# Stores of one weight's sums moved to SyncE's queue, and ScalarE taking over copies and scalings at the end of the plain tile

## The chip, the cores and the metric

The kernel runs on one core of one Trainium2 chip. A core has TensorE (PE, matmuls), VectorE (DVE), ScalarE (ACT), GpSimd (POOL) and SyncE (SP), each with an instruction stream of its own that is worked through in order. In this kernel SP and ACT issue the DMA transfers. The metric is the device time of one execution in microseconds (us), as the median of several runs.

## What is computed

Retention attention without softmax, and then a SwiGLU feed-forward block:

```python
q, k, v: (8, 8, 576, 64)          # batch, heads, tokens, head size
scores = scale * q @ k^T
ret = scores * gamma[h] ** (i - j)   for j <= i, else 0
attn = ret @ v
x = attn, heads beside each other:   (4608, 512)
g = x @ w_gate;  val = x @ w_val     # 512 x 1536 each
out = (silu(g) * val) @ w_out        # 1536 x 512
```

Everything is float32.

## The kernel before

**Attention.** Heads are worked on in pairs, 4 pairs (HP) to a batch entry, 32 pairs in all. `tick(t)` advances three pairs at once: it loads nothing itself, but transposes pair t (`transposes`), makes scores, states and masks of pair t - 1 (`scores`, `new_states`, `masked`), and values of pair t - 2 (`own_values`, `earlier_values`), which `to_x` writes into x, transposed. The parts on VectorE and ScalarE are put on the list `pieces` and taken off by `go_on(n)` between other work, so their place in the order of VectorE and ScalarE is set by hand. For a pair i,

- `light(i)` says that q is scaled ahead (by ScalarE, `scale_q`, L480), so that `to_x` only has to copy (ScalarE, L595 and L617); otherwise `to_x` multiplies by a table (VectorE, L597 and L611);
- `vector(i)` says that the keys are scaled by VectorE (L498) and that `even`, a copy of the states' first half out of PSUM, is made by VectorE (L571) for the pair before; otherwise ScalarE does both (L500, L571).

`needed(1)` is 14 and `needed(2)` is 22, so `light` holds for pairs 12 to 19, and `vector` for pairs 0, 10, 11 and 12.

**The plain tile.** The first 512 tokens go through the feed-forward block with plain matmuls: `up0` (12 blocks of 128 columns of w_gate and w_val, silu on ScalarE, product on VectorE) and `down0` (12 steps m, four matmuls each on the four PSUM banks A, B, C, E; L707). At m = 1, 3, 6 and 8 of `down0` the ticks 10 to 13 stand. They finish pairs 8 to 11. At the end `out0` copies the four banks (L712; A and B by ScalarE, C and E by VectorE) and stores them.

**The other four tiles.** Each has 1024 tokens and is multiplied by a fast scheme with 26 products (tables UP and DOWN) in place of 32 block products. Its operands are sums and differences of blocks of x, of the weights and of the hidden layer. One product is a *step*. `up_step(n, qd, i)` is step i of tile n with quarter qd of the hidden columns (NQ = 3). In tile 1 ("busy") the sums of the weights are made in passing (`w_sums`, GpSimd and ScalarE) and stored in DRAM by ScalarE's queue (L942), for the later tiles to fetch. The results of a step are read out of the bank by `reads`: a copy by ScalarE (L875), or a sum by VectorE (L878), and then silu (L954) and product (L957, L960, L961). A bank must have been read before the step that uses it next; the banks rotate by `rested`.

**Sums of x** (`x_sums`, L729 by way of `add`). Table UP has 21 of them. For tile 1 VectorE makes 14 ahead of step 0 (X_FIRST_OF_ALL: six at m = 9 and 10 of `down0`, the rest behind `out0`), and one more at each step from step 0. For the later tiles it is 8 ahead (X_FIRST). They are written to `xsum`, buffers that lie where earlier work had its own.

**Sums of w_out** (`out_sums(qd)`, L722 to L729). The 26 combinations of w_out's blocks (OUT_SUMS), 128 x 256 for each qd, are made and stored in DRAM tensors dn0 to dn25. GpSimd makes qd 0 and 1, and its stores are issued by SP. VectorE makes qd 2, and the first 18 of its stores are issued by ScalarE's queue (L790). Of its last eight, two that need no buffer follow there (L811), and six are issued by SP after the loop (`late_stores`, L792). Each qd is cut into nine groups of three stores. GpSimd's first 12 groups stand between the `up0` blocks. From m = 0 of `down0`, each m issues one group of GpSimd's (qd 1, groups 4 to 9) and then one of VectorE's (groups 1 to 9). A sum takes the first free buffer of its list; a buffer goes back to the end of the list when its sum is stored or no longer used, and whoever takes it again waits until the store has landed. VectorE's list (`vector_places`) has 22 buffers, of which the first eight (x0) are never given back.

A store waits on its queue until its sum is there, and every later instruction of that queue waits behind it.

Of the kernel before, what the change touches and what calls it, by code (L numbers as in the profile page):

```python
# [154 lines left out]
def kernel(  # L155
# [32 lines left out]
    nc = tc.nc  # L188
# [13 lines left out]
    TB = TW // 4  # L202
    NF = DF // P
    NQ = NF // 4
# [52 lines left out]
    def needed(n):  # L257

        last = (min(starts[n] + TW, NT) - 1) // S
        return last * HP + HP - 1 + 3  # L260
# [186 lines left out]

    def light(i):

        return needed(1) - 2 <= i < needed(2) - 2  # L450

    def vector(i):

        return i == 0 or 10 <= i <= needed(1) - 2

    def transposes(i):
        p = i % HP
        qk, kn, vt = loaded.pop(i)
        qT = early[i] if i < HP else qp.tile([P, S], F32, tag="qT", name="qT")
        st[i] = dict(qT=qT, kn=kn, v=vt)  # L460
        pieces = []

        copy = nc.scalar.copy if i else nc.vector.tensor_copy
        if i < HP:

            for n, (t, src, bank) in enumerate(((kT, kn, bankB), (qT, qk, bankA)) if i else ((qT, qk, bankA), (kT, kn, bankB))):
                for c in range(NFULL):
                    nc.tensor.transpose(bank[:, ts(c, P)], src[:, ts(c, P)], ident)
                for hl in range(2):
                    nc.tensor.matmul(bankC[half[hl], ts(n, L)], src[half[hl], CW : CW + D], ident[half[hl], half[hl]],  # L470
                                     start=True, stop=True, skip_group_check=True)
                copy(t[:, 0:CW], bank)
                copy(t[:, CW:S], bankC[:, ts(n, L)])
        else:
            if light(i):
                def scale_q():

                    src = qk[:, 0].rearrange("p (j r) d -> p r j d", r=2)
                    for r in range(2):
                        nc.scalar.activation(out=src[:, r], in_=src[:, r], func=AF.Copy, scale=piece[:, 2 * p + r : 2 * p + r + 1])  # L480
                pieces.append(scale_q)
            for n, t in enumerate((qT, kT)):
                pieces.append(lambda n=n, t=t: nc.vector.transpose(out=t, in_=qk[:, n].rearrange("p j d -> p (j d)")))

        every = slice(0, P)

        def keys():
            blocks = kn.rearrange("p (g d) -> p g d", d=D)
            if i < HP:
                parts = [(0, every, blocks[:, 0 : NC - 1 : 2]), (1, every, blocks[:, 1:NC:2]), (1, half[1], blocks[half[1], NC - 1])]  # L490
            elif whole(i):
                parts = [(0, every, blocks[:, 0:NFULL]), (1, every, blocks[:, NFULL:NC])]
            else:
                parts = [(hl, every, blocks[:, hl : 2 * NFULL : 2]) for hl in range(2)]
            for hl, rows, at in parts:
                scale = key[rows, 2 * p + hl : 2 * p + hl + 1]
                if vector(i) or 1 < i < HP:
                    (nc.vector if vector(i) else nc.gpsimd).tensor_scalar(out=at, in0=at, scalar1=scale, scalar2=None, op0=ALU.mult)  # L498
                else:
                    nc.scalar.activation(out=at, in_=at, func=AF.Copy, scale=scale)  # L500

        if light(i):
            return [lambda: (keys(), pieces[0]())] + pieces[1:]
        if vector(i) and i:
            return [lambda: None] + pieces + [keys]
        return [keys] + pieces

    straight, exchanged = [(slice(0, P), slice(0, P))], [(half[0], half[1]), (half[1], half[0])]
# [127 lines left out]
    pieces = []  # L636

    def tick(t, lo=HP, hi=NP, spread=False, then=None):
        go_on(len(pieces))
        if hi == HP:  # L640

            if lo <= t - 1 < hi:
                scores(t - 1, True)
                new_states(t - 1)
                for f in masked(t - 1):
                    f()
            if t + 1 == HP:
                split(0)
                rounding(0)
            if lo <= t - 2 < hi:  # L650
                own_values(t - 2)
            for f in transposes(t) if lo <= t < hi else ():
                f()
            if t + 1 == HP:
                rounding(1)
            if lo <= t - 2 < hi:
                earlier_values(t - 2)
                to_x(t - 2)[0]()
            return
        if lo <= t - 2 < hi:  # L660
            own_values(t - 2)
        if lo <= t - 1 < hi:
            new_states(t - 1)
        if lo <= t - 2 < hi:
            earlier_values(t - 2)
        if lo <= t - 1 < hi:
            scores(t - 1, t - 2 < lo)
        if lo <= t - 1 < hi and whole(t - 2) and not whole(t - 1):
            decay(slice(0, H), slice(0, H), half[1])
        copies, *masks = masked(t - 1) if lo <= t - 1 < hi else (lambda: None,)  # L670
        keys, *new = transposes(t) if lo <= t < hi else (lambda: None,)
        outputs = to_x(t - 2)[0] if lo <= t - 2 < hi else lambda: None
        if t - 2 >= 0 and light(t - 2):
            pieces.append(lambda: (copies(), keys(), outputs()))
        else:
            pieces.extend([lambda: (copies(), keys()), outputs])
        pieces.extend(masks)
        pieces.extend(new)
        if then:
            pieces.append(then)  # L680
        if not spread:
            go_on(len(pieces))
# [26 lines left out]

    def out0():  # L710
        for i, (bank, o) in enumerate(zip(banks, (hid0[f] for f in (0, 1, 4, 5)), strict=True)):
            (nc.vector.tensor_copy if i > 1 else nc.scalar.copy)(out=o, in_=bank)  # L712
            nc.sync.dma_start(out=out[i * P : (i + 1) * P, :], in_=o)


# [16 lines left out]
    dn_ops = [dr.tile([P, 768], F32, name=f"dn{i}") for i in range(N)]  # L732
# [16 lines left out]
    def out_sums(qd):  # L749
# [6 lines left out]
            if not any(p is q for q in x0_places):  # L756
                sum_places.append(p)

        eng, queue, sum_places = ((nc.vector, nc.scalar, vector_places) if qd + 1 == NQ else (nc.gpsimd, nc.sync, pool_places))

        def view(s):
            return w_dn[:, qd, s // 2, s % 2] if s < 8 else place[s]
# [21 lines left out]
        def do(k):  # L784
            e = events[k]
            if e[0] is None:
                _, slot, i = e
                to, what = dn_ops[i][:, qd * TB : (qd + 1) * TB], view(slot)
                if stored[k] < on_time:
                    queue.dma_start(out=to, in_=what)  # L790
                elif slot > 7:
                    late_stores.append(lambda: nc.sync.dma_start(out=to, in_=what))  # L792
            else:
                new = sum_places.pop(0)
                add(eng, e[1], view, new)
                if e[0] in place:
                    free(place[e[0]])
                place[e[0]] = new
            release(k)
# [3 lines left out]
        for g in range(0, N, 3):  # L803
            lo, hi = ends[g - 1] + 1 if g else 0, ends[min(g + 2, N - 1)] + 1

            def group(lo=lo, hi=hi):
                for k in range(lo, hi):
                    do(k)
                    if stored[k] + 1 == on_time and events[k][0] is None:
                        for _, slot, i in [e for e in events[k + 1 :] if e[0] is None and e[1] < 8]:  # L810
                            queue.dma_start(out=dn_ops[i][:, qd * TB : (qd + 1) * TB], in_=view(slot))  # L811

            r.append(group)
        return r
# [74 lines left out]

    x_ops = [op for line in up for op in line[3]]  # L890
    X_FIRST = 8
    X_FIRST_OF_ALL = 14

    def x_sums(n, lo, hi, vector):
        for op in x_ops[lo:hi]:
            add(nc.vector if vector or op[0] == "nad" else nc.gpsimd, op, x_view(n))
# [25 lines left out]
    def up_step(n, qd, i):  # L922
        label, opens, xslot, _, wslot, _, ops = up[i]
        busy = n == 1
        if qd == 0:
            first = X_FIRST_OF_ALL if busy else X_FIRST
            x_sums(n, first + i, first + i + 1, busy)
        if busy:
            if i > 1:
                w_sums(qd, i)  # L930
# [125 lines left out]
    for m, f in enumerate(down_order):  # L1056
        down0(f)
        go_on(6)
        if m in tick_at:
            tick(tick_at[m], HP, FIRST, tick_at[m] + 1 < needed(1))  # L1060
            go_on(1)
        if m == 5:
            first_sums(0, 0, 1)
        if m == 8:
            first_sums(0, 1, 4)
        if 8 < m < 11:
            x_sums(1, 3 * (m - 9), 3 * (m - 8), True)
        if groups:
            groups.pop(0)[1]()
        if last_groups:  # L1070
            last_groups.pop(0)()
    for store in late_stores:
        store()
    out0()
    x_sums(1, 6, X_FIRST_OF_ALL, True)
    done = FIRST

    def spread_tick(t):
# [56 lines left out]
```

## Time and profile before

| | us |
|---|---|
| median of 3 runs | 1063.14 (1060.99 to 1063.37) |
| the profiled execution | 1060.99 |
| its span, first to last instruction | 1059.3 |

The page's second part cuts the span into 40 slices of 26.5 us and gives each engine's busy tenths:

```profile
PE   6999999999999999999999999999999999999998
PEld 5554555788788888888888888888888888888887
DVE  5568789786878667454467787426375554244644
ACT  4456401232533211231322112232220022222110
POOL 2002358565455107622224038412250383122505
```

The plain tile's `down0` lies at 128 to 181 us (slices 5 and 6, counted from 0), and step 0 of tile 1 starts at 180.3 us. A row of the timeline gives the start, the length, the engine, the source line and the operation of one instruction or of several alike ("x3") and, in brackets, how long the engine had been idle and what ended it; "SPq" and "ACTq" are DMA issues of those queues. Line numbers are those of the kernel before.

### The profile page before, as it was taken

Reading aid. Unit: us, or ns where it says so; the run is one execution under the profiler, and the core shown is the slowest. Engines: PE = TensorE matmul, PEld = TensorE weight load, DVE = VectorE, ACT = ScalarE, POOL = GpSimd, SP = SyncE. Lnnn points to the kernel's source line nnn. Section 1 sums busy time; section 2 is a strip of 40 time slices with the busy share of each in tenths; the row PEclk is TensorE's granted clock in tenths of the full one; section 3 lists DMA queues with packets and bytes.
Section 4 is the critical chain, followed back from the end, with each engine's and each line's share of the span. In section 5 each row is a group of like instructions: output and inputs, shape, how many; then the busy total and the mean of one; then the engine's idle time right before and its main releaser. Section 6 shows DMA issues by size and latency. Waiting matters only on the chain.

```text
span 1059.3 us, 21436 instructions
## 1 busy us (share of the span) xinstructions
PE 1037.8 (98%) x8448; PEld 849.5 (80%) x8448; DVE 660.9 (62%) x1094; ACT 273.4 (26%) x579; POOL 390.9 (37%) x338
## 2 busy tenths in 40 slices
PE   6999999999999999999999999999999999999998
PEld 5554555788788888888888888888888888888887
DVE  5568789786878667454467787426375554244644
ACT  4456401232533211231322112232220022222110
POOL 2002358565455107622224038412250383122505
PEclk9999999999999999999999999999999999999999
DMA  9998786676768869765666777544554555555553
GB/s 263 248 258 239 191 247 216 185 199 187 196 175 215 265 166 257 199 149 175 190 183 172 212 197 212 152 147 141 153 179 150 154 187 151 151 155 160 181 159 99
DMA packets 305083, 199.09 MB, mean 188 GB/s; under 512 B 219992, under 2 KB 248664, under 8 KB 304984
## 3 DMA queue, kind: packets, MB, share of 16 engines
q1 hardware_dynamic: 270968, 159.02, 54.7%
q10 hardware_dynamic: 34016, 38.71, 10.9%
q8 instruction: 67, 1.10, 0.4%
q14 instruction: 32, 0.26, 0.1%
HBM read 157.56 MB, written 40.11 MB: 187 GB/s over the span
## 4 chain that ended last, share of the span: by engine, by line
PE 73%; DVE 5%; issue 1%; POOL 1%; DMA 1%; ACT 0%; SPq 0%; DVEq 0%; ACTq 0%; POOLq 0%
PE bankC L938 12%; PE bankE L938 11%; PE bankB L938 11%; PE bankA L938 11%; PE bankA L978 6%; PE bankE L978 6%; PE bankB L978 6%; PE bankC L978 6%; DVE rest L878 2%; PE outer L546 1%; PE outer L521 1%; PE inner L560 1%; PE inner L531 1%; DVE arena L960 1%; DVE arena L957 1%
## 5 line engine op out<-in xcount | busy, mean ns | idle before, releaser
L878 POOL TENSOR_TENSOR rest<-rest 128x512 f32<-128x512 f32 x56 | 79.2, 1419 | 297.7 <-DVE rest L878 279.2
L954 ACT ACTIVATE io<-rest 128x256 f32<-128x256 f32 x180 | 75.0, 416 | 343.7 <-DVE rest L878 292.1
L938 PE MATMUL bankA<-rest,arena 128*128 128x256 f32 x544 | 129.0, 380 | 1.0 <-DVE rest L878 1.0
L938 PE MATMUL bankC<-rest,arena 128*128 128x256 f32 x544 | 129.2, 380 | 0.5 <-DVE rest L878 0.5
L938 PE MATMUL bankB<-rest,arena 128*128 128x256 f32 x512 | 121.5, 380 | 2.0 <-POOL arena L907 1.6
L729 POOL TENSOR_TENSOR arena<-arena 128x512 f32<-128x512 f32 (+1 forms) x72 | 113.8, 1593 | 24.4 <-DMA up<-arena 11.5
L938 PE MATMUL bankE<-rest,arena 128*128 128x256 f32 x512 | 121.4, 380 | 0.6 <-DVE rest L878 0.6
L938 PEld LDWEIGHTS bankA<-rest,arena 128*128 128x128 f32 x544 | 102.9, 190 | 16.5 <-issue 1.4
L938 PEld LDWEIGHTS bankC<-rest,arena 128*128 128x128 f32 x544 | 102.8, 190 | 15.5 <-issue 1.2
L961 POOL TENSOR_TENSOR arena<-rest,io 128x256 f32<-128x256 f32 x72 | 51.8, 726 | 167.5 <-ACT io L954 167.5
L938 PEld LDWEIGHTS bankB<-rest,arena 128*128 128x128 f32 x512 | 96.9, 190 | 16.3 <-POOL arena L907 2.4
L938 PEld LDWEIGHTS bankE<-rest,arena 128*128 128x128 f32 x512 | 96.9, 190 | 14.6 <-DVE rest L878 1.0
L729 POOL TENSOR_TENSOR rest<-rest 128x256 f32<-128x256 f32 (+1 forms) x66 | 67.6, 1044 | 105.6 <-DVE rest L417 62.8
L878 DVE TENSOR_TENSOR rest<-bankC,rest 128x512 f32<-128x512 f32 x72 | 48.8, 686 | 67.4 <-PE bankC L938 47.2
L878 DVE TENSOR_TENSOR rest<-bankB,rest 128x512 f32<-128x512 f32 x72 | 48.9, 687 | 64.9 <-PE bankB L938 46.9
L878 DVE TENSOR_TENSOR rest<-bankE,rest 128x512 f32<-128x512 f32 x72 | 48.8, 686 | 64.4 <-PE bankE L938 46.3
L878 DVE TENSOR_TENSOR rest<-bankA,rest 128x512 f32<-128x512 f32 x72 | 48.8, 685 | 63.5 <-PE bankA L938 45.9
L957 DVE SCALAR_TENSOR_TENSOR arena<-rest,io 128x256 f32<-128x256 f32 x84 | 56.1, 673 | 11.7 <-ACT io L954 11.2
L978 PE MATMUL bankA<-arena 128*128 128x256 f32 x252 | 58.0, 380 | 1.4 <-DVE arena L729 1.4
L978 PE MATMUL bankB<-arena 128*128 128x256 f32 x252 | 58.3, 381 | 0.0
L978 PE MATMUL bankC<-arena 128*128 128x256 f32 x252 | 58.1, 380 | 0.0
L978 PE MATMUL bankE<-arena 128*128 128x256 f32 x252 | 57.9, 379 | 0.0
(184 smaller groups left out, 1626.6 us busy)
## 6 DMA issues: line engine op xcount, KB each, us to landing
arena<-up SPq DMA_DIRECT2D x234, 256.0 KB
arena<-dn SPq DMA_DIRECT2D x104, 384.0 KB
up<-arena ACTq DMA_DIRECT2D x78, 256.0 KB
out_dram<-rest SPq DMA_DIRECT2D x32, 256.0 KB
qk<-in_q_dram SPq DMA_DIRECT2D x108, 72.0 KB
qk<-in_k_dram SPq DMA_DIRECT2D x108, 72.0 KB
dn<-rest SPq DMA_DIRECT2D x58, 128.0 KB
rest<-in_moe_w_out_dram ACTq DMA_DIRECT2D x6, 1024.0 KB
```

What stands on the lines that cost most here:

```text
L521: m = nc.tensor.matmul(xo[half[hl ^ r * exchange(i)], c, r], s["v"][rows, at], ret[rows, r if whole(i) else hl, c], start=(c == 0), stop=( ...
L531: nc.tensor.matmul(z[half[hl], r, c], s["kn"][chunk(i, hl, 2 * c + r, i < HP)], s["v"][rows, at], start=True, stop=True, skip_group_check= ...
L546: nc.tensor.matmul(xr[half[hl]] if c + 1 == NC else xo[half[hl ^ c % 2 * exchange(i)], c // 2, c % 2], state[half[hl], c, :], s["qT"][half ...
L560: nc.tensor.matmul(sc[chunk(i, hl, 2 * c + r)[0], r if whole(i) else hl, c], kT[half[hl], at], qT[half[hl], at], start=True, stop=True, sk ...
L729: eng.tensor_tensor(out=dst, in0=srcs[0], in1=srcs[1], op=ALU.add if op[0] == "add" else ALU.subtract)
L878: eng.tensor_tensor(out=at(op[1]), in0=at(op[2]), in1=at(op[3]), op=ALU.add if op[0] == "add" else ALU.subtract)
L938: m = nc.tensor.matmul(b[:, gv * TB : (gv + 1) * TB], w[:, gv, ts(c, P)], rhs[:, c, :], start=(opens and gv == 0 and c == 0), stop=(c == 1 ...
L954: nc.scalar.activation(out=s, in_=src[:, 0:TB], func=AF.Silu, scale=-1.0 if negative else 1.0)
L957: return lambda: nc.vector.scalar_tensor_tensor(out=dst, in0=src[:, TB : 2 * TB], scalar=-1.0, in1=s, op0=ALU.mult, op1=ALU.mult)
L960: return lambda: nc.vector.tensor_tensor(out=dst, in0=src[:, TB : 2 * TB], in1=s, op=ALU.mult)
L961: nc.gpsimd.tensor_tensor(out=dst, in0=src[:, TB : 2 * TB], in1=s, op=ALU.mult)
L978: nc.tensor.matmul(b[:, m * TB : (m + 1) * TB], lhs[:, qd, ts(m, P)], w[:, qd], start=(opens and qd == 0 and m == 0), stop=(qd == NQ - 1), ...
```

## The change

- `light` holds from pair 8 in place of 12: q of pairs 8 to 11 is scaled by ScalarE, and their x is copied by ScalarE.
- `vector` holds for pair 0 alone: keys of pairs 10 to 12 are scaled by ScalarE, and `even` is copied by ScalarE in ticks 10 to 12.
- In ticks 10 and 11 (`late`) the order of the pieces is: the copy of `even` with the outputs, the masks, then keys and the scaling of q, then the transposes.
- `out0` copies all four banks by ScalarE.
- All stores of w_out's sums, VectorE's too, are issued by SP.
- For tile 1, 8 sums of x stand ahead of step 0 (at m = 9, 10 and 11) in place of 14; step i makes the (9 + i)th.

```diff
     def light(i):
-        return needed(1) - 2 <= i < needed(2) - 2
+        return needed(1) - 6 <= i < needed(2) - 2

     def vector(i):
-        return i == 0 or 10 <= i <= needed(1) - 2
+        return i == 0
...
         if light(i):
             return [lambda: (keys(), pieces[0]())] + pieces[1:]
-        if vector(i) and i:
-            return [lambda: None] + pieces + [keys]
         return [keys] + pieces
...
         outputs = to_x(t - 2)[0] if lo <= t - 2 < hi else lambda: None
-        if t - 2 >= 0 and light(t - 2):
+        late = needed(1) - 4 <= t < needed(1) - 2
+        if late:
+            pieces.append(lambda: (copies(), outputs()))
+        elif light(t - 2):
             pieces.append(lambda: (copies(), keys(), outputs()))
         else:
             pieces.extend([lambda: (copies(), keys()), outputs])
         pieces.extend(masks)
+        if late:
+            pieces.append(keys)
         pieces.extend(new)
...
         for i, (bank, o) in enumerate(zip(banks, (hid0[f] for f in (0, 1, 4, 5)), strict=True)):
-            (nc.vector.tensor_copy if i > 1 else nc.scalar.copy)(out=o, in_=bank)
+            nc.scalar.copy(out=o, in_=bank)
             nc.sync.dma_start(out=out[i * P : (i + 1) * P, :], in_=o)
...
-        eng, queue, sum_places = ((nc.vector, nc.scalar, vector_places) if qd + 1 == NQ else (nc.gpsimd, nc.sync, pool_places))
+        eng, sum_places = (nc.vector, vector_places) if qd + 1 == NQ else (nc.gpsimd, pool_places)
...
                 if stored[k] < on_time:
-                    queue.dma_start(out=to, in_=what)
+                    nc.sync.dma_start(out=to, in_=what)
...
                         for _, slot, i in [e for e in events[k + 1 :] if e[0] is None and e[1] < 8]:
-                            queue.dma_start(out=dn_ops[i][:, qd * TB : (qd + 1) * TB], in_=view(slot))
+                            nc.sync.dma_start(out=dn_ops[i][:, qd * TB : (qd + 1) * TB], in_=view(slot))
...
     X_FIRST = 8
-    X_FIRST_OF_ALL = 14
...
         if qd == 0:
-            first = X_FIRST_OF_ALL if busy else X_FIRST
-            x_sums(n, first + i, first + i + 1, busy)
+            x_sums(n, X_FIRST + i, X_FIRST + i + 1, busy)
...
-        if 8 < m < 11:
-            x_sums(1, 3 * (m - 9), 3 * (m - 8), True)
+        if m > 8:
+            x_sums(1, 3 * (m - 9), min(3 * (m - 8), X_FIRST), True)
...
     for store in late_stores:
         store()
     out0()
-    x_sums(1, 6, X_FIRST_OF_ALL, True)
     done = FIRST
```

## The prediction

> **What bounds the kernel now.** I read the shares of the page first, then the busy time by stretch, then the timeline around the end of the plain tile, then the waits.
>
> ```profile
> PE 1037.8 (98%) x8448; PEld 849.5 (80%) x8448; DVE 660.9 (62%) x1094; ACT 273.4 (26%) x579; POOL 390.9 (37%) x338
> ```
>
> TensorE is the bound: 21.5 us of the span are idle, and the change leaves TensorE's instructions as they are. What the change can win is idle time of PE, what it can lose is new idle time. The stretches around it (us busy for PE, PEld, DVE, ACT, POOL, then granted clock):
>
> ```profile
> 125.00:150.00 25.00, 25.00 (x448) 14.99 (x447) 19.62 (x47) 1.23 (x3) 10.41 (x13) 1.00 0.83 201
> 150.00:175.00 25.00, 24.91 (x252) 13.01 (x251) 22.43 (x49) 1.26 (x2) 23.18 (x30) 1.00 0.60 201
> 175.00:200.00 25.00, 23.14 (x92) 17.04 (x91) 24.74 (x29) 7.18 (x14) 12.88 (x9) 1.00 0.61 201
> ```
>
> PE is full until 175, and from 150 to 200 VectorE is full as well, while ScalarE is nearly empty. So the plain tile's end is PE's, the start of step one is VectorE's. The timeline shows the second:
>
> ```profile
> 180.32 1.89 PE L938 MATMUL bankA<-rest,arena 128*128 128x256 f32 x8
> ...
> 192.00 0.68 DVE L878 TENSOR_TENSOR rest<-bankA,rest 128x512 f32<-128x512 f32 x1
> ...
> 195.83 1.99 PE L938 MATMUL bankB<-rest,arena 128*128 128x256 f32 x8 [1.04 <-POOL arena L907]
> ...
> 198.40 1.99 PE L938 MATMUL bankE<-rest,arena 128*128 128x256 f32 x8 [0.57 <-DVE rest L878]
> ```
>
> Steps follow each other at 1.73 us (180.32, 182.05, 183.78 in the rows between). Step 4's bank A is complete at 187.23 + 1.89 = 189.1, but DVE reads it at 192.00, 2.9 us late, since sums of x and two bank copies stand ahead of it. Step 9 should start at 180.32 + 9 x 1.73 = 195.9 and starts at 198.40: 2.5 us are lost. That is the prize.
>
> The stores of w_out's sums now go out on two queues:
>
> ```profile
> 135.35 23.80 ACTq L790 DMA_DIRECT2D dn<-rest  x15
> ...
> 161.10 3.98 ACTq L790 DMA_DIRECT2D dn<-rest  x3
> 165.33 0.84 ACTq L811 DMA_DIRECT2D dn<-rest  x2
> ```
> ```profile
> 165.33 11.95 SPq L790 DMA_DIRECT2D dn<-rest  x15
> ```
> ```profile
> SPq L790 <- POOL rest L729: 14.1, 21, 1.9
> ```
>
> The ACT queue's 20 are VectorE's quarter (qd 2), issued as each sum is ready. SP's are GpSimd's, and SP sits waiting for GpSimd's sums, in order: 21 waits, 14.1 us. The 15 from 165.33 are GpSimd's 12th to 26th of qd 1 (dn11 first).
>
> **The change, part by part.**
>
> *ScalarE for VectorE.* DVE sheds the outputs of four ticks (the L597 and L611 rows from 164.52 to 165.45, 0.93 us each: 3.7), three copies of `even` (0.42: 1.2), the key scalings of pairs 10 and 11 (1.28 + 1.16) and of pair 12 (1.2), and two bank copies (0.68 each: 1.4), some 10 us. ACT takes them: per pair 0.35 (even), about 0.9 (x), 0.96 (keys), 0.95 (q scaled, L480), and 0.58 a bank, some 12.5 us in a stretch where it is busy 1.2 us of 25. Cost: nothing, hidden by that idle time. PE doesn't gain before 175 either, since it is full there. One thing slips: the first store of step one's weights (178.87, behind the copy of bank B) now stands behind the copy of bank E, which PE ends at 180.5: 1.7 us late. GpSimd's sum at 183.52 waits for it and is due at step 6 (190.7), so 5.9 us of cover take it in; without cover it costs 1.7.
>
> *Fewer sums of x ahead.* Six sums (0.69 us alone, 1.39 beside a busy GpSimd) leave the place before step 4's reading sum; with the bank copies that is 6 x 0.69 + 1.4 = 5.5 us against 2.9 us of lateness, so the 2.5 us can be won. They come back at steps 4 to 12: DVE then has 8 reading sums and 9 sums of x (17 x 0.69) and 5 products (0.42), 13.8 us, in 9 x 1.73 = 15.6 us. It fits if GpSimd doesn't stretch it; rows of 1.47 and 1.75 us in that stretch say that some are. Gain 0 to 2.5; I take 2.0.
>
> *All stores by SP.* This is where I expect the loss. In program order each m of the down loop issues one group of GpSimd's sums (qd 1, groups 4 to 9) and then one of VectorE's (groups 1 to 6), so on SP's queue VectorE's first group (dn14, dn2, dn9), ready at 135 to 139, now stands behind GpSimd's dn11, which is issued at 165.33. Why it matters: `vector_places` has 22 buffers. Counted through OUT_SUMS, VectorE's 23rd sum takes the first one freed, the one that held dn6 (third group), and must wait until dn6's store has landed; the 24th waits for dn3's. Now dn6 leaves on ACT at 146.57, and the 23rd sum runs unhindered at 163.76, the last of this row; behind it on DVE stand the masks and states of pair 11, which PE needs for the last tick:
>
> ```profile
> 161.37 3.23 DVE L729 TENSOR_TENSOR rest<-rest 128x256 f32<-128x256 f32 x4
> ...
> 165.45 0.68 DVE L567 TENSOR_TENSOR ret<-inner,near 128x512 f32<-128x512 f32 x1
> ...
> 167.94 0.69 PE L521 MATMUL outer<-ret,v 64*64 64x64 f32 x32
> ...
> 168.89 1.10 PE L546 MATMUL outer<-qT,state 64*64 64x64 f32 x32
> ```
>
> After: dn6 is the 14th store behind dn11 on SP (3 + 3 GpSimd + 3 + 3 GpSimd + dn1, dn6). Pace of a queue with nothing to wait for: 0.84/2 = 0.42 us (L811) to 3.19/6 = 0.53 (L792). 14 x 0.48 = 6.7: issued at 172.0; GpSimd's dn8, two ahead, is ready at about 170.8 (the second sum of the row at 169.39), so it asks for no more. Landing: a store issued at 150.09 let GpSimd go on at 153.1, 3.0 us (up to 4.65 for the larger store of 178.87 to 183.52). So the 23rd sum starts at 175.0 in place of 163.76. From there to PE's L546 it took 168.89 - 163.76 = 5.1 us, of which 0.9 were outputs that ACT now makes: 4.2. PE's L546 starts at 179.2, 10.3 us later; the two steps of down0 ahead of it end at 167.2 and nothing else can run on PE meanwhile. [...] Stall: 9.3, bounds 5 (0.42 a store, 2 us to land, GpSimd 2 us early) and 15 (0.75 a store, as the slowest of the L792 ones, and 4.65). Against a gain: below 0 only if the store isn't waited for.
>
> *Clock.* A pause of PE has a tail in this trace:
>
> ```profile
> 24.08 0.33 PE L470 MATMUL bankC<-ident,rest 64*64 64x64 f32 x4 [2.49 <-ACT kT L473]
> ```
> ```profile
> 25.00:30.00 5.00, 5.00 (x23) 2.30 (x20) 3.01 (x8) 3.16 (x6) 0.00 (x0) 0.66 0.89 302
> ```
>
> After 2.49 us of idle PE ran at 0.66 of its clock for 5 us: 0.34 x 5 = 1.7 us of work lost. I add 1.7 once (0 to 2.5). [...]
>
> **Sum**, from the profiled execution's 1060.99 us (span 1059.3 and 1.7 around it): + 9.3 (stall) + 1.7 (clock) - 2.0 (steps 7 to 9) = + 9.0, so 1070.0. The median of the runs shown is 2.15 above that execution: 1072; I say 1071, the pace of the stores being more likely nearer to 0.42.
>
> **Rivals.**
> 1. *The store is not in the way* (faster): dn6 lands before DVE comes to its 23rd sum. Price: - 2.5 and up to 1.1 more from the pauses at 218.47 and 222.72 (0.60 and 0.53 idle): about 1060. It decides if GpSimd has dn8 ready by about 160, ten us sooner than its row says. For it: GpSimd stood still for 14.1 us until 143.2, waiting for a store that was behind loads on SP. Against: those loads are still there, and from 143 it works without a break. Chance 0.08.
> 2. *Half of it* (within 0.3%, 1060.0 to 1066.3, about what a measurement can tell from no change): GpSimd is 3 us earlier, landing takes 2 us, the stall is 5, no clock is lost, 2.5 to 3.5 come back: 1065. Chance 0.13.
> 3. *Worse*: with 35 stores in a row the DMA is the bound, 0.75 a store: 14 x 0.75 + 4.65 puts the 23rd sum at 180.5, the stall at 15: 1078. For it: the last two of the six L792 stores took 0.56 and 0.75. Against: 0.60 to 0.61 DMA share in these stretches. Chance 0.14.
>
> **How the numbers follow.** My forecast, a stall of 6 to 12 us, has 0.65. With rival 3, slower by over 0.3% has 0.79; same 0.13; faster 0.08. The range 1064.5 to 1077 leaves out rival 1, a part of 2 and the end of 3.
>
> **What would show it.** Right: DVE's row of w_out sums has an idle time of some 10 us ended by the DMA of dn<-rest, L567's mask after it at about 176, PE idle for 8 us or more ahead of the last tick's matmuls (the `state` ones), a clock under 1.00 in the stretch behind it, and step 9 at 9 x 1.73 us behind step 0. No store of dn stands on ACT's queue. Wrong: the last tick's PE work at 168 to 170 as now; then the mapping of buffer to store is my error. If step 9 still comes late, the sums of x moved back are what VectorE can't fit.

## The result, and the profile after

The changed kernel takes 1068.27 us (median of 4 runs, 1066.08 to 1069.96) against 1062.84 for the kernel before beside it (4 runs, 1060.99 to 1063.37). The ratio is 1.0053, 95% interval 1.0029 to 1.0077: slower by 5.4 us, where 1071.0 was forecast. A second comparison of the same two kernels, made with the experiments, gave 1.0053 again (1.0035 to 1.0072). The profiled execution is the one of 1066.08 us, span 1064.4, 5.1 us over that of the profile before.

The page's shares:

```profile
PE 1039.6 (98%) x8448; PEld 851.7 (80%) x8448; DVE 650.6 (61%) x1063; ACT 284.4 (27%) x610; POOL 389.3 (37%) x338
```

VectorE has 31 instructions fewer, ScalarE 31 more: the takeover is there. TensorE does the same 8448 matmuls in 1.8 us more busy time, so part of the loss isn't idle time. The stretches (us busy for PE, PEld, DVE, ACT, POOL, then granted clock, DMA share, GB/s):

```profile
150.00:175.00 25.00, 19.68 (x232) 11.01 (x232) 11.30 (x22) 1.04 (x4) 20.45 (x27) 0.92 0.60 199
175.00:200.00 25.00, 25.00 (x94) 16.81 (x91) 13.30 (x18) 8.78 (x18) 6.58 (x6) 0.94 0.55 194
200.00:225.00 25.00, 24.44 (x113) 20.83 (x112) 23.77 (x30) 6.29 (x13) 20.50 (x14) 1.00 0.75 198
```

From 150 to 175 PE is idle for 5.3 us where it was full, VectorE has fallen from 22.4 busy to 11.3, and the clock is 0.92 and then 0.94. VectorE does less here, and still PE waits for it. The timeline says why:

```profile
154.78 22.95 SPq L793 DMA_DIRECT2D dn<-rest  x39
165.54 1.02 PE L710 MATMUL bankE<-rest,arena 128*128 128x512 f32 x2
170.53 0.42 DVE L732 TENSOR_TENSOR rest<-rest 128x256 f32<-128x256 f32 x1 [12.90 <-DMA dn<-rest]
170.88 0.68 DVE L565 TENSOR_TENSOR ret<-inner,near 128x512 f32<-128x512 f32 x1
171.75 1.14 PE L519 MATMUL outer<-ret,v 64*64 64x64 f32 x32 [5.18 <-DVE ret_last L573]
173.49 1.98 PE L544 MATMUL outer<-qT,state 64*64 64x64 f32 x32
175.40 2.07 PE L710 MATMUL bankA<-rest,arena 128*128 128x512 f32 x2
187.11 1.89 PE L939 MATMUL bankA<-rest,arena 128*128 128x256 f32 x8
196.01 0.69 DVE L881 TENSOR_TENSOR rest<-bankA,rest 128x512 f32<-128x512 f32 x1 [10.27 <-PE bankA L939]
```

SP issues 39 stores of dn from 154.78 to 177.7. The single sum at 170.53 is VectorE's 23rd: it has waited for 12.90 us, for a dn store to land. Behind it stand the masks (L565) and `ret_last`, and PE, out of work since 166.6, waits for them for 5.18 us. After the pause matmuls run slower: L544 takes 1.98 us where it took 1.10, two of L710 take 2.07 where they take 1.02 at 165.54. The granted clock is 0.50 from 173.4 to 177.4, 0.84 in the 2 us behind that and 1.00 from 179.4.

With the matmuls of the two traces laid side by side, the 5.1 us are made up so:

| where | us |
|---|---|
| start-up, before 31 us | - 1.45 |
| from there to L544, 168.89 before and 173.49 now: the pause | + 6.05 |
| L544 to step 0 (180.32 and 187.11): the clock | + 2.2 |
| step 0 to step 9 (18.08 us before, 15.54 now): VectorE's and GpSimd's lateness is gone | - 2.54 |
| later pauses of PE, 0.56 and 1.51 us ahead of steps 13 and 22, less those of before (the rest of the 5.1) | + 0.85 |

The start-up is the same code, and in the second profile of this kernel it is only 0.42 us earlier, so the first row is a matter of the execution.

### The profile page after: what moved, and what is told of

It is laid out like the page before. It is cut to its first block, busy times and chain, and to the rows that moved or that the text cites. A ratio compares the mean times of both kernels' runs of the same rounds, so it can differ in the third digit from the quotient of the medians.

```text
span 1064.4 us, 21448 instructions
## 1 busy us (share of the span) xinstructions
PE 1039.6 (98%) x8448; PEld 851.7 (80%) x8448; DVE 650.6 (61%) x1063; ACT 284.4 (27%) x610; POOL 389.3 (37%) x338
## 4 chain that ended last, share of the span: by engine, by line
PE 84%; DVE 5%; POOL 3%; issue 3%; DMA 2%; SPq 1%; ACT 1%; ACTq 0%; DVEq 0%; POOLq 0%
PE bankC L939 11%; PE bankE L939 11%; PE bankA L939 11%; PE bankB L939 11%; PE bankA L979 6%; PE bankB L979 6%; PE bankC L979 6%; PE bankE L979 6%; PE bankA L698 2%; PE bankC L698 2%; PE outer L544 2%; PE bankB L698 2%; PE bankE L698 2%; PE outer L519 2%; DVE rest L881 2%
```

## The experiments

All times are medians beside runs of the kernel before on the same chip, which took 1061.23, 1062.2 and 1062.41 us in the three sets; ratios are to those.

**1. VectorE's stores back on ScalarE's queue, all else as changed.**

```diff
-        eng, sum_places = (nc.vector, vector_places) if qd + 1 == NQ else (nc.gpsimd, pool_places)
+        eng, queue, sum_places = (nc.vector, nc.scalar, vector_places) if qd + 1 == NQ else (nc.gpsimd, nc.sync, pool_places)
...
-                    nc.sync.dma_start(out=to, in_=what)
+                    queue.dma_start(out=to, in_=what)
```

> The changed kernel with VectorE's stores of w_out's sums back on ScalarE's queue. Theory (the 23rd sum waits for dn6's store behind GpSimd's stores on SyncE, PE's last tick stalls, the clock falls): no idle of PE ahead of the last tick, clock 1.00 at 150 to 200, time 1059 to 1061.5, below the kernel before. Rival A (the spread sums of x or ScalarE's new work cost the time): 1066 to 1069 as the changed kernel. Rival B (crowded DMA on SyncE's queue, whatever the buffer): as the theory, 1059 to 1061.5.

Measured: 1067.43 us, ratio 1.0058 (1.0042 to 1.0075). That is the time of the changed kernel, and what rival A had said (1066 to 1069); my theory and rival B, which had 1059 to 1061.5, missed. The wait for dn6 is gone, and another has come, by way of ScalarE's new work. From the timeline:

```profile
163.41 2.25 ACTq L793 DMA_DIRECT2D dn<-rest  x3
166.33 0.81 ACTq L814 DMA_DIRECT2D dn<-rest  x2
167.24 0.37 ACT L569 COPY even<-inner 128x256 f32<-128x256 f32 x1 [5.87 <-DMA dn<-rest]
167.64 0.69 DVE L565 TENSOR_TENSOR ret<-inner,near 128x512 f32<-128x512 f32 x1 [4.46 <-ACT even L569]
172.09 1.97 PE L544 MATMUL outer<-qT,state 64*64 64x64 f32 x32 [2.39 <-DVE state L580]
```

ScalarE's copy of `even`, the work that it has taken over, stands in ScalarE's order behind five stores, and those wait in that same order. VectorE had ended its sums at 163.2, 4.46 us ahead of the mask at 167.64, so the last of these stores no longer waited for a sum; what the profile names as the end of ScalarE's idle time is the landing of a store. VectorE's masks wait for the copy, PE for the masks (1.27 us at L519) and the state. What was to be a control of one part joined two parts of the change that don't go together; run 5 takes that apart.

**2. All stores by SP alone, on the kernel before.**

```diff
-        eng, queue, sum_places = ((nc.vector, nc.scalar, vector_places) if qd + 1 == NQ else (nc.gpsimd, nc.sync, pool_places))
+        eng, queue, sum_places = ((nc.vector, nc.sync, vector_places) if qd + 1 == NQ else (nc.gpsimd, nc.sync, pool_places))
```

> The kernel before with VectorE's stores on SyncE's queue and nothing else. Theory: the stall appears, 5 to 8 us idle of PE at the last tick, 2 us of clock, nothing won back: 1068 to 1072. Rival A: as the kernel before, within 1.5 us of it. Rival B: as the theory.

Measured: 1069.87 us, ratio 1.0082 (1.0065 to 1.0099). The timeline, and then the clock of the two stretches:

```profile
174.82 0.44 DVE L729 TENSOR_TENSOR rest<-rest 128x256 f32<-128x256 f32 x1 [10.70 <-DMA dn<-rest]
176.97 1.13 PE L521 MATMUL outer<-ret,v 64*64 64x64 f32 x32 [8.61 <-DVE ret_last L575]
```
```profile
150.00:175.00 25.00, 18.36 (x172) 9.05 (x171) 12.78 (x27) 0.00 (x0) 22.73 (x29) 0.94 0.54 180
175.00:200.00 25.00, 22.89 (x130) 15.25 (x131) 19.84 (x37) 4.98 (x9) 5.89 (x4) 0.85 0.62 213
```

The one line of the queue makes the same wait, with a longer pause of PE, 8.61 us in the profiled execution (1073.34 us, the longest of the six), and costs 8.6 us in the median. Nothing comes back: step 9 is at 209.51, 17.68 us behind step 0 (191.83).

**3. Another buffer for the 23rd sum.** A buffer that is overwritten by a later sum is taken again first. The 23rd sum then takes the one of dn5, whose late store has not read it yet, so in this run a third of dn5 holds another sum; the work is the same.

```diff
                 if e[0] in place:
-                    free(place[e[0]])
+                    if qd + 1 == NQ and not any(place[e[0]] is q for q in x0_places):
+                        sum_places.insert(0, place[e[0]])
+                    else:
+                        free(place[e[0]])
```

> The changed kernel, all stores on SyncE, but the one freed buffer that is never stored is taken again first, so that the 23rd sum finds a fresh buffer and only the 24th (behind the masks) waits for dn6. Theory: the stall is gone although the queue is as crowded: 1059 to 1062. Rival A: 1066 to 1069. Rival B: 1066 to 1069, since the stores are as late as before.

Measured: 1060.27 us, ratio 0.9993 (0.9981 to 1.0006). No pause of PE at the last tick, clock 0.999, step 0 at 178.72:

```profile
166.34 0.69 PE L519 MATMUL outer<-ret,v 64*64 64x64 f32 x32
167.29 1.10 PE L544 MATMUL outer<-qT,state 64*64 64x64 f32 x32
```

All stores still stand on SP's queue, so it isn't their number that costs.

**4. The spread of the sums of x alone, on the kernel before.**

```diff
-            first = X_FIRST_OF_ALL if busy else X_FIRST
-            x_sums(n, first + i, first + i + 1, busy)
+            x_sums(n, X_FIRST + i, X_FIRST + i + 1, busy)
```

(and, as in the change, nothing behind `out0` and two more at m = 11)

> The kernel before with 8 sums of x ahead of step one in place of 14 and nothing else. Theory: step 9 no longer late by 2.5 us but VectorE fuller at steps 4 to 12: between -2.5 and +1 us against before, 1060.5 to 1064. Rival A: slower by 3 us or more.

Measured: 1060.7 us, ratio 0.9999 (0.9987 to 1.0012): no change that could be told. VectorE reads step 4's bank 3.5 us sooner than before (188.48), and step 9 comes on time, at 195.13, 15.5 behind step 0. About half of what that earns goes again at steps 13, 18 and 22; step 22 starts 41.07 us behind step 0, against 42.40 in the kernel before (PE's idle times in the timeline):

```profile
202.83 1.97 PE L936 MATMUL bankE<-rest,arena 128*128 128x256 f32 x8 [0.56 <-DVE rest L878]
212.19 1.99 PE L936 MATMUL bankA<-x_odd,arena 128*128 128x256 f32 x8 [0.49 <-POOL arena L906]
220.66 1.97 PE L936 MATMUL bankC<-rest,arena 128*128 128x256 f32 x8 [1.27 <-DVE rest L878]
```

**5. ScalarE's takeover alone, on the kernel before** (the changes of `light`, `vector`, the ticks and `out0`; stores and sums of x as before).

```diff
-        return needed(1) - 2 <= i < needed(2) - 2
+        return needed(1) - 6 <= i < needed(2) - 2
...
-        return i == 0 or 10 <= i <= needed(1) - 2
+        return i == 0
```

> The kernel before with only ScalarE's part: ticks 8 to 11 light (q scaled by ScalarE in front of its product, keys by GpSimd, the two copies to x by ScalarE) and all four evictions of the early output by ScalarE; VectorE's tile's stores stay on ScalarE's queue and 14 sums of x stay ahead. My theory: the added work of ScalarE stands in its order behind stores that wait for VectorE's sums and for a place in the DMA queue, so ScalarE's copy (L569 or near it) in the last tick waits as in e1, PE pauses 3 to 6 us at about 165 to 172, and the time is 1064 to 1069 us. Rival, the takeover is free as I had forecast, and e1's loss comes from the spread of x's sums: 1059 to 1062 us, no pause of PE over 1.5 us between 150 and 175.

Measured: 1064.67 us, ratio 1.0021 (1.0007 to 1.0034): my theory, at its lower end. (The keys, which the expectation gives to GpSimd, are scaled by ScalarE, L500. What it calls a wait for a place in the DMA queue is seen as this: VectorE had ended its sums at 163.0, stores were still issued at 165.22 and 166.35, and the profile names the landing of a dn store as the end of ScalarE's 6.11 us.) The timeline shows the same row as in run 1:

```profile
166.35 0.83 ACTq L814 DMA_DIRECT2D dn<-rest  x2
167.28 0.37 ACT L569 COPY even<-inner 128x256 f32<-128x256 f32 x1 [6.11 <-DMA dn<-rest]
168.63 0.69 PE L519 MATMUL outer<-ret,v 64*64 64x64 f32 x32 [1.66 <-DVE ret_last L573]
172.08 1.97 PE L544 MATMUL outer<-qT,state 64*64 64x64 f32 x32 [2.34 <-DVE state L580]
```

PE idles 1.66 + 2.34 = 4.0 us. Steps 0 to 9 then follow without lateness (185.88 to 201.41, 15.53 us) although 14 sums of x stand ahead.

**6. The changed kernel with the 10th sum's buffer taken again first.** That value is never stored, so nobody waits for it; the 23rd sum gets the last unused buffer, the 24th the one of dn6.

```diff
+                kept.append(what)
...
                 if e[0] in place:
-                    free(place[e[0]])
+                    old = place[e[0]]
+                    if qd + 1 == NQ and not any(old is q for q in x0_places + kept):
+                        sum_places.insert(0, old)
+                    else:
+                        free(old)
```

> The changed kernel; VectorE's sums of the last quarter take again first the buffer whose value was never stored (that of the 10th sum). The 23rd sum then takes the last unused buffer and waits for nothing; the 24th, one group later, takes the one of dn6. My theory: what is behind the 24th sum is only sums of x for step one onwards, which have slack, so it costs at most 1 us: 1059.5 to 1062.5 us, PE without a pause over 1 us before its state product L544. Rival, the wait only moves: the 24th sum holds the sums of x until about 171 and step 0 to 4 come late: 1063 to 1066 us.

Measured: 1060.9 us, ratio 0.9984 (0.997 to 0.9997). The timeline:

```profile
155.10 24.89 SPq L794 DMA_DIRECT2D dn<-rest  x42
162.68 0.69 DVE L565 TENSOR_TENSOR ret<-inner,near 128x512 f32<-128x512 f32 x1 [2.13 <-ACT even L569]
169.15 0.69 PE L519 MATMUL outer<-ret,v 64*64 64x64 f32 x32
170.09 1.10 PE L544 MATMUL outer<-qT,state 64*64 64x64 f32 x32
173.20 0.90 DVE L732 TENSOR_TENSOR rest<-rest 128x256 f32<-128x256 f32 x1 [7.17 <-DMA dn<-rest]
```

The store is as late as before and VectorE still waits for it, 7.17 us. But the waiting sum now stands behind the masks, PE goes through the tick without a pause, and L544 keeps its 1.10 us. A wait of the same kind costs some 7 us in one place of VectorE's order and nothing in the next.

**7. Run 2 with the buffers of run 6**: the kernel before, all stores by SP, no takeover.

> The kernel before with the last quarter's stores on SP's queue, as in e2, and the same order of buffers as in e6. My theory: on SP's queue the stores harm by the one buffer that VectorE waits for, and by nothing else: 1060 to 1064 us, where e2 took 1069.9. Rival, a crowded queue of SP as such (loads and stores behind the stores come late): 1066 to 1070 us.

Measured: 1063.6 us, ratio 1.0006 (0.9992 to 1.002), where run 2 had 1.0082. The timeline:

```profile
171.06 1.15 PE L546 MATMUL outer<-qT,state 64*64 64x64 f32 x32 [0.48 <-DVE state L582]
172.68 1.09 DVE L729 TENSOR_TENSOR rest<-rest 128x256 f32<-128x256 f32 x1 [1.68 <-DMA dn<-rest]
```

On SP's queue the stores harm by that wait and by nothing that can be measured; the interval leaves room for 2 us.

**8. Run 6 with 14 sums of x ahead, as before.**

```diff
+    X_FIRST_OF_ALL = 14
...
-            x_sums(n, X_FIRST + i, X_FIRST + i + 1, busy)
+            first = X_FIRST_OF_ALL if busy else X_FIRST
+            x_sums(n, first + i, first + i + 1, busy)
```

> e6 with 14 sums of x ahead of step one, as in the kernel before, in place of 8 and one a step. In e3 VectorE idled for 5.3 us just before it read step 4's bank, and was then late at some steps from 9 on (pauses of PE of 0.7 to 1.5 us). If those 6 sums fill that idle time, the gain of spreading them isn't needed and the pauses at steps 12 to 22 fall away: 1057.5 to 1060.5 us. Rival: the sums wait for x's loads or for buffers, hold VectorE's read of step 4, and cost what they save: 1060.5 to 1063.5 us.

Measured: 1060.08 us, ratio 0.9977 (0.9964 to 0.999). It is faster than both kernels, by 0.23% than before and by some 0.75% than the changed one. The two stretches that the prediction read show where the room is: VectorE, busy 22.43 and 24.74 us of 25 in the kernel before, now has 17.99 and 22.77.

```profile
150.00:175.00 25.00, 24.91 (x251) 12.90 (x250) 17.99 (x27) 3.31 (x11) 23.27 (x29) 1.00 0.63 207
175.00:200.00 25.00, 24.51 (x101) 18.69 (x100) 22.77 (x29) 8.56 (x16) 11.37 (x9) 1.00 0.77 247
```

Against run 6 it is 0.8 us, within the intervals: whether 8 or 14 stand ahead can't be told apart.

**9. One store moved.** In the changed kernel, dn6's store of VectorE's quarter alone goes back to ScalarE's queue.

```diff
-                    nc.sync.dma_start(out=to, in_=what)
+                    (nc.scalar if qd + 1 == NQ and i == 6 else nc.sync).dma_start(out=to, in_=what)
```

> The changed kernel; of VectorE's 20 stores that moved, dn6's alone goes back to ScalarE's queue, and no buffer is given in another order. My theory, that the loss is the wait of the 23rd sum for this one store: 1060 to 1063 us, as e6, and no pause of PE over 1 us ahead of L544. Rival, that other stores behind GpSimd's on SP's queue cost something too, or that ScalarE is held up by this one store: 1064 to 1068 us.

Measured: 1061.31 us, ratio 0.9991 (0.9977 to 1.0006), beside 1.0053 for the changed kernel in the same set. One DMA issue of 0.36 us, in another queue, takes some 6.6 us off. The rows of that store and of the next sum that waits:

```profile
144.61 0.36 ACTq L793 DMA_DIRECT2D dn<-rest  x1
174.25 0.83 DVE L732 TENSOR_TENSOR rest<-rest 128x256 f32<-128x256 f32 x1 [8.71 <-DMA dn<-rest]
```

dn6 leaves at 144.61 instead of 168.37. The 24th sum waits for dn3's store, 8.71 us, and that costs nothing, as in run 6.

**10. The changed kernel with 14 sums of x ahead** (the edit of run 8), and **11. the changed kernel again**.

> The changed kernel with 14 sums of x ahead of step one, so without its third part. If the spread is worth nothing with the pause in place, as e4 showed without it: the same as the run of the changed kernel beside it, within 1 us (1067 to 1069). If the spread costs time where steps come late, as the difference of e1 (ratio 1.0058) to e5 (1.0021) would have it: 2 to 3 us faster than the changed kernel (1064.5 to 1066.5). If it earns the 2.0 us of my forecast: 2 us slower (1070).

> The changed kernel once more, for a comparison on the same chip with the two runs beside it: 1066 to 1069.5 us, ratio 1.004 to 1.007. A wait of VectorE of 10 to 14 us for a dn store ahead of its last tick's masks, and PE idle for 4 to 7 us at L519.

Measured: 1067.08 us, ratio 1.0047 (1.0029 to 1.0065), and 1068.04 us, 1.0053 (1.0035 to 1.0072): the spread is worth nothing that could be told beside the pause either. From the timeline of run 10, and then of run 11:

```profile
172.88 0.42 DVE L732 TENSOR_TENSOR rest<-rest 128x256 f32<-128x256 f32 x1 [12.95 <-DMA dn<-rest]
174.10 1.13 PE L519 MATMUL outer<-ret,v 64*64 64x64 f32 x32 [5.24 <-DVE ret_last L573]
```
```profile
171.54 0.49 DVE L732 TENSOR_TENSOR rest<-rest 128x256 f32<-128x256 f32 x1 [12.72 <-DMA dn<-rest]
172.81 1.13 PE L519 MATMUL outer<-ret,v 64*64 64x64 f32 x32 [5.22 <-DVE ret_last L573]
```

Three profiles, three times the same pause of 5.2 us. The gap between run 1 and run 5 (1.0058 and 1.0021), which differ by the spread alone, is thereby not explained by it. They were measured in different sets, their profiled executions hardly differ (1065.27 and 1064.99 us, PE's two pauses 3.66 and 4.0 us together), and it stays open.

## Why the prediction came out as it did

**The stall: right in place and cause.** The 23rd sum waits for dn6's store, the 14th behind dn11 on SP, and the last tick's masks stand behind it. Runs 2, 6, 7 and 9 show it from four sides: the queue alone makes the stall, another buffer takes it away with the queue left as it is, with or without the takeover, and so does the one store. That the DMA is not the bound (rival 3) is shown by run 3 and run 6, where a row of stores as long (42 in the line of run 6) costs nothing (ratios 0.9993 and 0.9984). Rival 1 fell with the wait of 12.90 us. Rival 2 had a landing of 2 us and GpSimd 3 us sooner, near to what came (2.16 us, and dn11 out 4.1 us sooner, 1.45 of it start-up), but no loss of clock and 2.5 to 3.5 us won back; the 2.2 of the clock and the 1.7 won back are what sets the result apart from it. Its stall of 5 us is a wrong sum: its own terms give 165.33 - 3 + 6.7 + 2 + 4.2 - 168.89 = 6.3.

**Its size: too large, 9.3 forecast and 6.05 measured.** That is the term of the sum that was mis-sized. Worked out by the prediction's own chain:

| term | forecast | measured | us |
|---|---|---|---|
| dn11's issue, with 1 us taken off for GpSimd | 164.33 | 161.24 | - 3.1, of which 1.45 is the start-up |
| 14 stores | 14 x 0.48 = 6.7 | 168.37 - 161.24 = 7.13 | + 0.4 |
| dn6's issue to the sum | 3.0 | 170.53 - 168.37 = 2.16 | - 0.8 |
| the sum to L544 | 4.2 | 173.49 - 170.53 = 2.96 | - 1.2 |

The pace held. The landing was taken from a row that held more than a landing: what let GpSimd go on was seen 3.0 us behind one issue, the store's own share is 2.2. The chain behind the sum was taken from VectorE's time beside a busy PE and a row of outputs, and was shorter. The 9.3 is 10.3 less 1 us for a GpSimd that may be sooner, an estimate for which no run shows a reason. GpSimd was sooner by more than that: net of the start-up dn11 leaves 165.33 - 161.24 - 1.45 = 2.6 us sooner. That isn't the chance of one execution: runs 10 and 11 issue dn11 at 163.54 and 162.42, with a start-up 0.85 us later and 0.42 earlier than in the profile of before, which makes 2.6 and 2.5. Why GpSimd is sooner by that much stays open.

The lower bound of 5 is mis-summed as well: 0.42 a store, 2 us to land and GpSimd 2 us early give 165.33 - 2 + 5.9 + 2 + 4.2 - 168.89 = 6.5. The 6.05 measured lies under that, by the shorter chain behind the sum, and only just in the 6 to 12 that had 0.65.

**Clock: + 1.7 forecast, + 2.2 measured**, over L544 and the three steps of `down0` behind it: rows of 1.10 and 1.02 us that became 1.98 and 2.07, at a granted clock of 0.50 for 4 us behind the 5.18 us of idle time. The forecast had one row to go by, 0.66 for 5 us behind 2.49.

**Steps 7 to 9: - 2.0 forecast, - 2.54 there and + 0.85 later, so - 1.7: near in number, by luck in part.** I put it down to fewer sums of x ahead. Run 4 shows that part alone to bring step 9 on time, but half of it goes again by step 22 and the time shows nothing of the rest; runs 8 and 10 show the kernel to be no slower without it. ScalarE's takeover brings step 9 forward by itself: with 14 sums ahead it stands 15.53 us behind step 0 in run 5 and, where PE doesn't pause, 16.20 in run 8 (196.38 less 180.18), against 17.66 in run 7 (200.20 less 182.54). Run 8 against run 7, which differ by the takeover, is 0.9977 against 1.0006, some 3 us. The prediction had counted only the two bank copies of the takeover here; of the rest it said that PE doesn't gain before 175, "since it is full there". So the rest was valued in the stretch in which it stands, while VectorE's time comes free behind it. What makes up the 1.7 in the changed kernel, where both parts and the pause meet, isn't shown: run 6, the same parts without the pause, has step 9 on time (15.72) and step 22 at 42.44 us behind step 0, no sooner than the kernel before.

**"Cost: nothing, hidden by that idle time" of ScalarE** holds only because the stores leave its queue. The prediction took ScalarE's 1.26 us of busy time in 25 for room. It was no room: the queue stood there in order with stores that waited. With them left on it the takeover costs 2.2 us (run 5, interval 0.7 to 3.6). The rows that said so were in the profile of before: a store queue of 23.8 us on ScalarE, and behind it an activation ahead of which ScalarE had stood idle until a store landed.

```profile
159.20 0.63 ACT L916 ACTIVATE arena<-arena 128x512 f32<-128x512 f32 x1 [29.66 <-DMA dn<-rest]
```

So the two main parts of the change belong together (run 6: 0.9984), and the one buffer undoes their gain.

**SP's 21 waits.** Of the rows of before, that of SP's waits for GpSimd's sums, 14.1 us, is the one that decided. Run 2's 8.6 us go with it, and so does run 9, where one issue of 0.36 us makes some 6.6 us. What a queue decides here is behind whose waits a store stands.

What would have shown it wrong did not appear: the wait is there (12.90 us, said to be some 10), the mask at 170.88 (said 176), a clock of 0.92 and 0.94, and step 9 at 9 x 1.73 behind step 0. One sign of being right missed its size, with the stall: PE idles 5.18 us, not 8 or more.

## What to carry to other kernels

ScalarE, busy 1.26 us of 25, had no room: its queue held DMA issues that waited, and ahead of the copy that it took over it stood idle, 5.87 us in run 1 and 6.11 in run 5. So read the releasers of an engine's idle time before its share. When a store changes queues, go through the list of buffers and ask which instruction takes the stored buffer next and what stands behind it; take again first a buffer whose value is never stored, or leave that one store where it was. And judge a wait by what follows it on its engine: 12.9 us ahead of the last tick's masks cost 6 to 8, 7.2 us one group later cost nothing.

## What was unexpected of the hardware

Matmuls as slow as in the changed kernel came after less idle time than its pause of 5.18 us. In run 5 PE idled 1.66 us, ran L519 in its usual 0.69 us, idled another 2.34 us, and L544 then took 1.97 us and two of L710 2.07 us. The length of the last pause alone doesn't decide it: in run 10 a single pause of 2.50 us, in the down steps of tile 1, left the clock at 1.00 and the steps behind it at 1.73 us. The row and the two stretches:

```profile
354.85 2.83 PE L981 MATMUL bankB<-arena,rest 128*128 128x256 f32 x12 [2.50 <-DMA arena<-dn]
```
```profile
354.00:358.00 4.00, 3.15 (x15) 2.82 (x16) 2.27 (x7) 1.88 (x7) 0.00 (x0) 1.00 1.00 393
358.00:362.00 4.00, 4.00 (x20) 3.54 (x19) 3.41 (x6) 0.30 (x1) 0.00 (x0) 1.00 0.80 264
```

The pause of 2.49 us at the start of the kernel before, almost as long, was followed by 0.66 from 25 to 30. What makes the difference isn't shown: no run here was made for it.
